# An attention and a feed-forward layer on one core: weight conversion for the first pass moved wholly into the attention stage

## The chip, the cores and the metric

The kernel runs on one core of a Trainium2 chip. The metric is the device time of one execution in microseconds; the time before is the median of three runs. The engines are called as in the profile: PE (TensorE, with PEld for its weight loads), DVE (VectorE), ACT (ScalarE), POOL (GpSimd) and SP (SyncE, which issues all the DMAs here).

## The reference

Random-feature linear attention for 8 batches, 8 heads, 576 tokens and head size 64 is followed by a feed-forward layer over 4608 tokens (model width 512, inner width 2048), all in float32.

```python
def phi(x):
    proj = einsum('bhsd,df->bhsf', x, w_phi)            # 128 features
    proj = proj - max(abs(proj), axis=-1)
    return concatenate([exp(proj), exp(-proj)], axis=-1)
q_p, k_p = phi(q), phi(k)
kv  = einsum('bhsf,bhsd->bhfd', k_p, v);  z = sum(k_p, axis=2)
x   = einsum(q_p, kv) / (einsum(q_p, z) + 1e-6)         # to (4608, 512)
h   = x @ w_in
out = (h * tanh(softplus(h))) @ w_out
```

In the kernel's inputs `w_in` and `w_out` stand as 64-bit words, and the kernel makes float32 pairs (a high and a low part) of them itself: this is the weight conversion.

## The kernel before

**An order written by hand.** Every piece of work is put into a list with a time, `at(time, fn, ...)`, and the list is sorted once. The times set only the order in which each engine, and SP's DMA queue, gets its instructions. What an engine does when is decided on the chip by semaphores.

**Attention.** 36 units of 512 columns each on the key side (`k_*`) and the query side (`q_*`). One step of `STEP` holds key unit u+4 and query unit u. A unit is projected on PE (`k_proj`, `q_proj`, into PSUM tile pp), centred on DVE (`center`: a reduction of the maximum and a subtraction, L204 and L205), and exponentiated on ACT (`k_exp`; for queries after a transpose on PE, `q_turn`, then `q_exp`). `k_sum` adds up kv on PE and `k_store` copies a finished pair out (ACT). `q_num` multiplies by kv on PE; `q_norm` on DVE adds 1e-6 to the denominator (L309), inverts it (L310) and multiplies (L311), each twice a unit; `q_out` transposes on PE, `q_store` copies on ACT and sends x to DRAM (`x_spill`). The last four query units have no key unit beside them; their steps are `TAIL_STEP`.

**Feed-forward.** x is read back in nine chunks of 512 tokens (`x_load`); `x_sum` forms four differences (DVE, L349), and `x_block` makes seven blocks with a high part (ACT, L357) and a low part (DVE, L358). A step (`n`, 72 in all) is one chunk with one of eight pairs of weight blocks (`fp`, numbered 0 to 7): `ff_in` (PE, L374, 42 matmuls), `winograd` (DVE), `mish` and `g_hi` (ACT), `g_lo` (DVE, L415), and `ff_out` (PE, L438, 24 matmuls) for the step before. A segment (`segs`) is a chunk with several pairs in a row; at its end `drain` adds to or starts a partial sum in DRAM. The x blocks are made anew for every segment. `NFIRST` = 4 chunks have their first four pairs in two segments of two steps, the other chunks in one of four.

**Weight conversion.** A piece (`weight_ops`) is a quarter of one pair's `w_in` or `w_out`: five bit operations (absolute, clamp, shift, sign, scale: DVE, the absolute on ACT where not `quiet`), a few POOL operations, one ACT copy (`hi`, L161), and POOL's low part. Eight pieces (pairs 0 and 1) are converted during the attention and stay in SBUF; the eight of pairs 2 and 3 right after it, without pause, into tiles of the pool `late`, whose memory is the attention's until that ends (`close`); the sixteen of pairs 4 to 7 after those, into DRAM (`in_spill`, `out_spill`), from where `again` and `again_out` load them for the second pass. `begin` is the time in the list at which the feed-forward stage proper starts.

Of the kernel before, what the change touches and what calls it, by code (L numbers as in the profile page):

```python
# [16 lines left out]
P = 128  # L17
# [12 lines left out]
SMALL, LARGE = 2.0 ** -15, 1.875 * 2.0 ** 16 - 2.0 ** -7  # L30

LEAD = 4
LEAD_STEP, STEP, TAIL_STEP = 3.0, 7.4, 5.7
FFSTEP = 10.6
HALF = 4
EARLY, SOON, LATER = 22.0, 0.0, 9.0
NFIRST = 4
AHEAD = 2
NXC = 10

# [5 lines left out]
def attention_then_mish(ctx, tc, qT, kT, va, w_phi, w_in, w_out, out):  # L46
# [21 lines left out]
    out_spill = {(fp, k): tc.dram_tile([P, 2, DM], F32, name=f"out_spill_{fp}_{k}")  # L68
                 for fp in range(HALF, NFP) for k in range(2)}

    win, wout, piece = {}, {}, {}

# [26 lines left out]
    def weight_ops(kind, fp, k, quiet):  # L99

        key = (kind, fp, k)
        eng = nc.gpsimd

        def w():
            return piece[key][1][:, 0:4].rearrange("p b m -> p (b m)")

        def absolute():
            words = piece[key][0]
            w8 = ffn.tile([P, 8, P], F32, tag="w8", name=f"w8_{kind}_{fp}_{k}", bufs=2)
            piece[key].append(w8)  # L110
            if quiet:
                nc.vector.tensor_scalar(w().bitcast(U32), words[:, 1], 0x7FFFFFFF, None, op0=ALU.bitwise_and)
            else:
                nc.scalar.activation(w(), words[:, 1].bitcast(F32), AF.Abs)

        def clamp():
            nc.vector.tensor_scalar(w(), w(), LARGE, SMALL, op0=ALU.min, op1=ALU.max)  # L117

        def shift():
            wu = w().bitcast(U32)  # L120
            nc.vector.tensor_scalar(wu, wu, 3, 0x3FFFFFF8, op0=ALU.logical_shift_left, op1=ALU.bitwise_and)

        def sign():
            wu = w().bitcast(U32)
            nc.vector.scalar_tensor_tensor(wu, piece[key][0][:, 1], 0xC0000000, wu, op0=ALU.bitwise_and,  # L125
                                           op1=ALU.bitwise_or)
# [12 lines left out]
        def place():  # L139
            if fp < HALF:  # L140
                resident(fp)
                return win[fp][:, k] if kind == "in" else wout[fp][:, k]
            st = ffn.tile([P, 2, 7 * P], F32R, tag="wst", name=f"wst_{kind}_{fp}_{k}", bufs=1)
            if kind == "in":
                return st.rearrange("p h (b m) -> p h b m", m=P)
            return st[:, :, :DM]

        def total():
            eng.tensor_tensor(w(), w(), piece[key][2], op=ALU.add)  # L149

        def sums(i):
            w8 = piece[key][1]
            a21, a11, a22, a12, s1, s2, s3, s4 = (w8[:, b] for b in range(8))
            o, x, y, op = ((s1, a21, a22, ALU.add), (s2, s1, a11, ALU.subtract), (s3, a11, a21, ALU.subtract),
                           (s4, a12, s2, ALU.subtract))[i]
            eng.tensor_tensor(o, x, y, op=op)  # L156

        def hi():
            dst = place()
            piece[key].append(dst)  # L160
            nc.scalar.copy(dst[:, 0], piece[key][1][:, 1:8] if kind == "in" else w())  # L161

        def lo():
            dst = piece[key][3]
            eng.tensor_sub(dst[:, 1], piece[key][1][:, 1:8], dst[:, 0].bitcast(F32))
            done()

        def rest():
            dst = piece[key][3]
            eng.tensor_sub(w(), w(), dst[:, 0].bitcast(F32))  # L170

        def lo_out():
            dst = piece[key][3]
            eng.tensor_tensor(dst[:, 1], w(), piece[key][2], op=ALU.add)
            done()

        def done():
            dst = piece.pop(key)[3]
            pieces_left.discard(key)
            if fp >= HALF:  # L180
                nc.sync.dma_start(in_spill[fp, k] if kind == "in" else out_spill[fp, k], dst.bitcast(F32))

        ops = [(0.0, absolute), (0.9, clamp), (1.35, shift), (1.8, sign), (2.5, scale)]
        rest_ops = [(2.2, low)]
        if kind == "in":
            rest_ops += [(1.45, total)] + [(0.65, lambda i=i: sums(i)) for i in range(4)] + [(1.6, hi), (2.3, lo)]
        else:
            rest_ops += [(1.3, hi), (1.45, rest), (1.45, lo_out)]
        return ops, rest_ops
# [72 lines left out]
            nc.scalar.copy(kv[p // NHP, p % NHP], kv_ps.pop(p))  # L262


    q_live, x_live, num_live, turned, out_live = {}, {}, {}, {}, {}

    def q_load(n):
        q_live[n] = att.tile([P, 512], F32, tag="qraw", name=f"qraw_{n}", bufs=3)
# [20 lines left out]
    def q_num(n):  # L289
# [3 lines left out]
        for i in range(2):  # L293
# [7 lines left out]
                               start=(t == j == s == 0), stop=(s == 1))  # L301
            num_live[n, i] = ps

    def q_norm(n):
        x = x_live[n]
        for i in range(2):
            ps = num_live.pop((n, i))
            r = att.tile([P, 2, 2], F32, tag="r", name=f"r{i}_{n}", bufs=3)
            nc.vector.tensor_scalar(r, ps[:, :, :, D], 1e-6, None, op0=ALU.add)  # L309
            nc.vector.reciprocal(r, r)  # L310
            nc.vector.tensor_tensor(x[:, i].rearrange("p t (j d) -> p t j d", d=D), ps[:, :, :, :D],  # L311
                                    r.unsqueeze(3).broadcast_to([P, 2, 2, D]), op=ALU.mult)
# [28 lines left out]
    def x_sum(s, i):  # L341
# [130 lines left out]

    for u in range(NU):
        t, after = base(u - LEAD), base(u - LEAD + 1)
        at(t - 1.5 * STEP, k_load, u)
        at(t - 0.8 * STEP, v_load, u)
        at(t, k_proj, u)
        at(t + 0.95, k_center, u)
        at(t + 3.4, k_exp, u)
        at(after + (3.85 if after >= 0 else 0.9), k_sum, u)  # L480
        at(after + (6.3 if after >= 0 else 3.5), k_store, u)
        t, after, end = base(u), base(u + 1), base(u + 2)
        at(t - 1.2 * STEP, q_load, u)
        at(t + 0.95, q_proj, u)
        at(t + 4.9, q_center, u)
        for j in range(2):
            tail = STEP - TAIL_STEP if u + 1 >= NU - LEAD else 0
            at(after + 6.45 + 0.45 * j - tail, q_turn, u, j)
            at(after + 6.9 + 1.2 * j - tail, q_exp, u, j)
        at(end + 1.9, q_num, u)  # L490
        at(end + 3.35, q_norm, u)
        tail = STEP - TAIL_STEP if u + 2 >= NU - LEAD else 0
        at(end + 6.0 - tail, q_out, u)
        at(end + 6.5 - tail, q_store, u)

    begin = base(NU + 2) + 1.0
# [6 lines left out]
    at(begin - 0.5, close)  # L503

    def t_of(n):
        return begin + 5.6 + (n - AHEAD) * FFSTEP if n >= AHEAD else begin - 13.0 + 5.5 * n

    clock = 6.0
    for i, pc in enumerate(pieces):
        quiet = i >= 8  # L510
        if i == 8:
            clock = max(clock, begin + 5.0)
        at(clock - 12.0, weight_load, *pc)
        bits, sums = weight_ops(*pc, quiet)
# [81 lines left out]
```

## Time and profile before

| | us |
|---|---|
| median of three runs | 1110.99 (1110.9 to 1111.02) |
| the profiled execution | 1111.28 |
| its span, first to last instruction | 1109.5 |
| PE busy | 1057.6 |
| DVE busy | 749.3 |
| ACT busy | 489.0 |
| POOL busy | 245.6 |

Busy time is a sum over stages which have different limits. In the 40 slices of the page (27.7 us each) the attention fills about the first eleven; the slices after it up to the 25th hold the conversion beside the feed-forward steps, and from the 26th on POOL does nothing. In a line of a group the last part is the idle time of the engine just before the group, with what ended it. Rows of the timeline have the start, the length, and in brackets the idle time before.

### The profile page before, as it was taken

To read this page: it belongs to the slowest core of one execution; us is meant where nothing else is said; L and a number is where in the kernel's file an instruction comes from. 1 tells how busy PE (TensorE), PEld (TensorE's weight loads), DVE (VectorE), ACT (ScalarE), POOL (GpSimd) and SP (SyncE) were. 2 spreads that over 40 slices of the span, in tenths; PEclk is the share of its full clock that TensorE was granted. 3 is DMA by queue.
4 is the path that set the end of the run, shared out by engine and by line. 5 is a ranking of instruction groups with operands and counts; after the bars stand their busy time and mean duration, and the time that the engine had idled before them with its cause. 6 is when DMAs were issued, how large, how long until landed. Compare 5 with 4: busy or idle time off the path is not lost.

```text
span 1109.5 us, 25630 instructions
## 1 busy us (share of the span) xinstructions
PE 1057.6 (95%) x11200; PEld 958.3 (86%) x11200; DVE 749.3 (68%) x1166; ACT 489.0 (44%) x804; POOL 245.6 (22%) x198
## 2 busy tenths in 40 slices
PE   7899999999888889999999999999999999999998
PEld 6799999999776778879898989999999999999997
DVE  4788878888858987898846757545545545545543
ACT  4666667665544434343435335333323323323331
POOL 0222211111027766543425443000000000000000
PEclk9999999999989989999999999999999999999999
DMA  5535544454223326554341533850230330230221
GB/s 160 170 107 181 162 153 164 151 169 144 87 80 111 131 98 214 214 199 145 121 148 58 175 121 130 338 208 19 95 115 19 96 114 19 96 114 19 96 76 38
DMA packets 62815, 140.29 MB, mean 126 GB/s; under 512 B 4976, under 2 KB 27632, under 8 KB 59376
## 3 DMA queue, kind: packets, MB, share of 16 engines
q1 hardware_dynamic: 62704, 138.66, 36.5%
q8 instruction: 88, 1.44, 0.5%
q14 instruction: 23, 0.19, 0.0%
HBM read 94.60 MB, written 44.04 MB: 125 GB/s over the span
## 4 chain that ended last, share of the span: by engine, by line
PE 52%; DVE 12%; DMA 2%; ACT 2%; POOL 2%; issue 2%; SPq 0%; DVEq 0%; POOLq 0%; ACTq 0%
PE o L438 27%; PE h L374 25%; DVE xc L358 5%; DMA x<-x_spill 2%; DVE xs L349 1%; DVE gl L415 1%; POOL w_in L156 1%; ACT gh L410 1%; DVE u L398 1%; DVE part L446 1%; DVE w_in L125 0%; ACT u L405 0%; POOL t_in L137 0%; DVE w_in L117 0%; POOL w_in L149 0%
## 5 line engine op out<-in xcount | busy, mean ns | idle before, releaser
L374 PEld LDWEIGHTS h<-xc,win 128*128 128x128 f32 x3024 | 383.8, 193 | 37.6 <-issue 15.1
L374 PE MATMUL h<-xc,win 128*128 128x256 f32 x3024 | 392.3, 285 | 20.2 <-DVE u L394 11.9
L438 PE MATMUL o<-wout,gh 128*128 128x512 f32 x1152 | 362.2, 396 | 2.9 <-ACT gh L410 2.9
L438 PEld LDWEIGHTS o<-wout,gh 128*128 128x128 f32 x1152 | 209.9, 191 | 40.0 <-ACT gh L410 3.2
L438 PE MATMUL o<-wout,gl 128*128 128x512 f32 x576 | 226.3, 393 | 4.2 <-DVE gl L415 4.2
L379 ACT COPY p<-h 128x256 f32<-128x256 f32 x72 | 26.8, 372 | 304.1 <-PE h L374 304.1
L386 DVE TENSOR_TENSOR u<-h,p 128x256 f32<-128x256 f32 x72 | 30.4, 422 | 183.8 <-ACT p L379 183.8
L438 PEld LDWEIGHTS o<-wout,gl 128*128 128x128 f32 x576 | 109.6, 190 | 29.1 <-DVE gl L415 5.0
L415 DVE TENSOR_TENSOR gl<-u,gh 128x1024 fp32r<-128x1024 f32 x72 | 93.0, 1292 | 29.1 <-ACT gh L410 29.1
L403 ACT ACTIVATE u<-h 128x256 f32<-128x256 f32 x72 | 27.7, 384 | 149.5 <-PE h L374 144.0
L213 PE MATMUL kvps<-v,e_k 128*64 128x65 f32 x2560 | 83.4, 224 | 4.8 <-ACT e_k L243 4.2
L213 PEld LDWEIGHTS kvps<-v,e_k 128*64 128x64 f32 x2560 | 79.7, 140 | 6.0 <-ACT e_k L243 4.6
L358 DVE TENSOR_TENSOR xc<-x,xc 128x512 fp32r<-128x512 f32 x88 | 75.1, 871 | 11.4 <-ACT xc L357 11.2
L213 PE MATMUL num<-kv,e_q 128*64 128x65 f32 x2304 | 78.4, 223 | 3.4 <-ACT e_q L287 2.7
L213 PEld LDWEIGHTS num<-kv,e_q 128*64 128x64 f32 x2304 | 71.5, 137 | 9.8 <-ACT e_q L287 5.3
L410 ACT CAST gh<-u 128x1024 fp32r<-128x1024 f32 x72 | 75.8, 1052 | 2.2
L287 ACT ACTIVATE e_q<-dt 128x512 f32<-128x512 f32 x144 | 75.5, 613 | 0.1
L398 DVE TENSOR_TENSOR u<-h,u 128x512 f32<-128x512 f32 x72 | 49.3, 685 | 38.5 <-ACT u L403 35.5
L242 ACT ACTIVATE e_k<-e_k 128x1024 f32<-128x1024 f32 x36 | 38.1, 1058 | 76.7 <-DVE e_k L205 76.7
L204 DVE TENSOR_REDUCE m_k<-pp_k 128x8 f32<-128x1024 f32 x36 | 44.0, 1222 | 40.6 <-PE pp_k L198 40.3
L405 ACT ACTIVATE u<-u 128x768 f32<-128x768 f32 x72 | 61.1, 849 | 3.0 <-DVE u L398 3.0
L358 DVE TENSOR_TENSOR xc<-xs,xc 128x512 fp32r<-128x512 f32 x66 | 55.5, 861 | 2.0 <-ACT xc L357 2.0
(62 smaller groups left out, 1166.5 us busy)
## 6 DMA issues: line engine op xcount, KB each, us to landing
x<-x_spill SPq DMA_DIRECT2D x44, 512.0 KB, 5.6
o_part<-part SPq DMA_DIRECT2D x13, 1024.0 KB, 4.8
part<-o_part SPq DMA_DIRECT2D x13, 1024.0 KB, 7.7
v<-va SPq DMA_DIRECT2D x32, 325.0 KB, 3.2
kraw<-kT SPq DMA_DIRECT2D x36, 256.0 KB, 3.9
qraw<-qT SPq DMA_DIRECT2D x36, 256.0 KB, 3.8
x_spill<-xs SPq DMA_DIRECT2D x36, 256.0 KB, 2.7
out<-part SPq DMA_DIRECT2D x36, 256.0 KB, 2.0
```

The costliest lines, as they stand in the source:

```text
L204: nc.vector.tensor_reduce(m, ps, axis=AX.X, op=ALU.max, apply_absolute_value=True)
L213: nc.tensor.matmul(ps[rows], lhsT[:, rows], rhs[h], start=start, stop=stop, skip_group_check=True)
L242: nc.scalar.activation(e[:, :, 1, :], e[:, :, 0, :], AF.Exp)
L287: nc.scalar.activation(e[:, s, :], ps, AF.Exp, scale=2.0 * s - 1.0)
L358: nc.vector.tensor_sub(blk[:, 1], src, blk[:, 0].bitcast(F32))
L374: nc.tensor.matmul(ps, w, x, start=(i in (0, 2) and m == 0), stop=(m == 5), skip_group_check=True)
L386: nc.vector.tensor_tensor(u2, ps[:, 0, 1], u_live[n][0], op=ALU.add)
L398: nc.vector.tensor_tensor(u[:, 1:3], ps[:, 1], u2.unsqueeze(1).broadcast_to([P, 2, CH]), op=ALU.add)
L405: nc.scalar.activation(u[:, 1:4], u[:, 1:4], AF.Mish)
L410: nc.scalar.copy(gh, u_live[n][3])
L415: nc.vector.tensor_tensor(gl, u_live.pop(n)[3], g_live[n][0].bitcast(F32), op=ALU.subtract)
L438: nc.tensor.matmul(ps, g, w, start=(first and f == k == 0), stop=(last and f == 1 and k == 2))
```

## The change

Four things, and new times for the order:

1. All sixteen pieces of pairs 0 to 3 are converted during the attention, one per 14.91 of the list's time. Pairs 2 and 3 go through DRAM and are loaded at `begin` by `again` and `again_out`. The pieces of pairs 4 to 7 start at `begin` + 40.03, with 7.91 between two (before: 9). `NFIRST` is 2, so that there are 20 segments in place of 22.
2. The differences of the first two segments and the low parts of the first segment's blocks are made on POOL.
3. `q_den` on ACT adds 1e-6 (two small instructions a unit); DVE's two reciprocals become one.
4. The last four query units have an order of their own (`T_AT`): a unit's operations follow one another more closely, so that the units overlap differently. In the other steps `k_proj` comes between the two halves of `q_turn`, and `q_den` ahead of `k_exp` on ACT.

```diff
-LEAD_STEP, STEP, TAIL_STEP = 3.0, 7.4, 5.7
+LEAD_STEP = 3.07
+STEP = 7.43
+TAIL_STEP = 5.73
+K_AT = (-0.57, 0.6, 3.04, 3.85, 4.24)
+Q_AT = (0.95, 4.18, 6.45, 6.55, 1.9, 3.04, 5.9, 6.5)
+T_AT = (0.95, 2.0, 4.9, 5.3, 9.0, 10.38, 12.6, 13.1)
+JOIN = 1.0
+PRE = (11.72, 6.53)
+CONV = (12.64, 14.91)
+WORD_AT = 4.77
+X0_AT = (40.59, 30.15)
+RESUME = 40.03
-EARLY, SOON, LATER = 22.0, 0.0, 9.0
-NFIRST = 4
+LATER = 7.91
+NFIRST = 2
...
-                for fp in range(HALF, NFP) for k in range(2)}
+                for fp in range(2, NFP) for k in range(2)}
...
-            if fp < HALF:
+            if fp < 2:
                 resident(fp)
...
-            if fp >= HALF:
+            if fp >= 2:
                 nc.sync.dma_start(in_spill[fp, k] if kind == "in" else out_spill[fp, k], dst.bitcast(F32))
...
+    def q_den(n):
+        r = r_live[n] = att.tile([P, 2, 2, 2], F32, tag="r", name=f"r_{n}", bufs=3)
+        for i in range(2):
+            nc.scalar.activation(r[:, i], num_live[n, i][:, :, :, D], AF.Copy, bias=1e-6)
+
     def q_norm(n):
         x = x_live[n]
+        r = r_live.pop(n)
+        nc.vector.reciprocal(r, r)
         for i in range(2):
             ps = num_live.pop((n, i))
-            r = att.tile([P, 2, 2], F32, tag="r", name=f"r{i}_{n}", bufs=3)
-            nc.vector.tensor_scalar(r, ps[:, :, :, D], 1e-6, None, op0=ALU.add)
-            nc.vector.reciprocal(r, r)
...
-        nc.vector.tensor_tensor(o, a, b, op=ALU.subtract)
+        (nc.gpsimd if s < 2 else nc.vector).tensor_tensor(o, a, b, op=ALU.subtract)
...
-        nc.vector.tensor_sub(blk[:, 1], src, blk[:, 0].bitcast(F32))
+        (nc.vector if s else nc.gpsimd).tensor_tensor(blk[:, 1], src, blk[:, 0].bitcast(F32), op=ALU.subtract)
...
-        at(end + 1.9, q_num, u)
-        at(end + 3.35, q_norm, u)
+        at(end + a[4], q_num, u)
+        at(end + a[5], q_den, u)
+        at(end + a[5] + 0.05, q_norm, u)
...
-        quiet = i >= 8
-        if i == 8:
-            clock = max(clock, begin + 5.0)
+        quiet = i >= 4 * HALF
+        if i == 4 * HALF:
+            clock = max(clock, begin + RESUME)
+        if i < 4 * HALF:
+            clock = CONV[0] + CONV[1] * i
...
+    for fp in (2, 3):
+        at(begin + 0.1 if fp == 2 else begin + 7.6, again, fp)
+        at(begin + 7.4 + 0.1 * fp, again_out, fp)
```

More of the change, by code (lines that the diff above doesn't have):

```diff
@@ L66, in attention_then_mish @@
     in_spill = {(fp, k): tc.dram_tile([P, 2, 7, P], F32, name=f"in_spill_{fp}_{k}")
-                for fp in range(HALF, NFP) for k in range(2)}
+                for fp in range(2, NFP) for k in range(2)}
     out_spill = {(fp, k): tc.dram_tile([P, 2, DM], F32, name=f"out_spill_{fp}_{k}")
-                 for fp in range(HALF, NFP) for k in range(2)}
+                 for fp in range(2, NFP) for k in range(2)}
     win, wout, piece = {}, {}, {}
@@ L262, in k_store @@
             nc.scalar.copy(kv[p // NHP, p % NHP], kv_ps.pop(p))
-    q_live, x_live, num_live, turned, out_live = {}, {}, {}, {}, {}
+    q_live, x_live, num_live, turned, out_live, r_live = {}, {}, {}, {}, {}, {}
     def q_load(n):
@@ L474, in attention_then_mish @@
         t, after = base(u - LEAD), base(u - LEAD + 1)
+        lead = after < 0
         at(t - 1.5 * STEP, k_load, u)
         at(t - 0.8 * STEP, v_load, u)
[L477 to L481, printed above, removed]
-        t, after, end = base(u), base(u + 1), base(u + 2)
+        at(t + K_AT[0], k_proj, u)
+        at(t + K_AT[1], k_center, u)
+        at(t + K_AT[2], k_exp, u)
+        at(after + (0.9 if lead else K_AT[3]), k_sum, u)
+        at(after + (3.5 if lead else K_AT[4]), k_store, u)
+        t, after, end = base(u), base(u + 1), base(u + 2)
+        cut = STEP - TAIL_STEP
+        after -= cut if u == NU - LEAD - 1 else 0.0
+        close_by = end - (cut if u >= NU - LEAD - 2 else 0.0)
+        if u >= NU - LEAD:
+            after = end = close_by = t
+        a = T_AT if u >= NU - LEAD else Q_AT
         at(t - 1.2 * STEP, q_load, u)
-        at(t + 0.95, q_proj, u)
-        at(t + 4.9, q_center, u)
+        at(t + a[0], q_proj, u)
+        at(t + a[1], q_center, u)
         for j in range(2):
-            tail = STEP - TAIL_STEP if u + 1 >= NU - LEAD else 0
-            at(after + 6.45 + 0.45 * j - tail, q_turn, u, j)
-            at(after + 6.9 + 1.2 * j - tail, q_exp, u, j)
-        at(end + 1.9, q_num, u)
-        at(end + 3.35, q_norm, u)
[L492 to L496, printed above, removed]
+            at(after + a[2] + 0.45 * j, q_turn, u, j)
+            at(after + a[3] + 1.2 * j, q_exp, u, j)
+        at(end + a[4], q_num, u)
+        at(end + a[5], q_den, u)
+        at(end + a[5] + 0.05, q_norm, u)
+        at(close_by + a[6], q_out, u)
+        at(close_by + a[7], q_store, u)
+    begin = base(NU + 2) + JOIN
     def close():
@@ L505, in t_of @@
     def t_of(n):
-        return begin + 5.6 + (n - AHEAD) * FFSTEP if n >= AHEAD else begin - 13.0 + 5.5 * n
+        return begin + 5.6 + (n - AHEAD) * FFSTEP if n >= AHEAD else begin - PRE[0] + PRE[1] * n
     clock = 6.0
     for i, pc in enumerate(pieces):
-        quiet = i >= 8
-        if i == 8:
-            clock = max(clock, begin + 5.0)
+        quiet = i >= 4 * HALF
[3 more added lines that the diff above has]
+            clock = CONV[0] + CONV[1] * i
         at(clock - 12.0, weight_load, *pc)
@@ L515, in attention_then_mish @@
         for delay, op in bits:
-            at(clock - 5.0 + delay, op)
+            at(clock - WORD_AT + delay, op)
         for cost, op in sums:
@@ L519, in attention_then_mish @@
             clock += cost
-        clock += EARLY if i < 8 else SOON if i < 16 else LATER
+        clock += LATER
     for s, (sc, fps) in enumerate(segs):
         n = steps.index((s, sc, fps[0], True, fps[0] == fps[-1]))
-        t = t_of(n - 2) if n >= AHEAD + 2 else begin - (45, 20)[s]
+        t = t_of(n - 2) if n >= AHEAD + 2 else begin - (X0_AT[0], 20)[s]
         at(t + 1.0, x_load, s, sc)
@@ L527, in attention_then_mish @@
             at(t + 5.5 + 0.7 * i, x_sum, s, i)
-        t = t_of(n - 1) if n >= AHEAD + 2 else begin - (30, 3.9)[s]
+        t = t_of(n - 1) if n >= AHEAD + 2 else begin - (X0_AT[1], 3.9)[s]
         for b in range(7):
```

2 lines of the change are left out of this document (1 added, 1 removed).

## The prediction

> **What bounds the kernel now.** I read the page first, then the chain of work that ended last, then busy time by stage, and last single stretches in order of time.
>
> ```profile
> span 1109.5 us, 25630 instructions
> PE   7899999999888889999999999999999999999998
> DVE  4788878888858987898846757545545545545543
> PEclk9999999999989989999999999999999999999999
> ```
>
> PE is the bound over most of the span, but it falls to 8 in slices 11 to 15 (27.7 us each), where DVE reaches 9 in slice 14 and the granted clock dips to 8 in slices 12 and 15. What a feed-forward step costs undisturbed is in the end of the chain:
>
> ```profile
> 1082.23 2.15 PE h L374 x18
> 1087.13 2.87 PE h L374 x24
> 1092.75 2.15 PE h L374 x18
> ```
>
> The second halves of two successive steps start at 1082.23 and 1092.75: 10.52 us a step, all of it PE. Step 2, the first after the seam, and the seam's own marks:
>
> ```profile
> 271.88 1.16 PE L198 MATMUL pp_q<-w_phi,qraw 64*128 64x128 f32 x16
> 292.54 1.16 PE L198 MATMUL pp_q<-w_phi,qraw 64*128 64x128 f32 x16
> 319.32 0.73 PE L438 MATMUL o<-wout,gh 128*128 128x512 f32 x2 [2.91 <-ACT gh L410]
> 321.98 0.79 PE L438 MATMUL o<-wout,gl 128*128 128x512 f32 x1 [1.93 <-DVE gl L415]
> 329.57 0.64 PE L374 MATMUL h<-xc,win 128*128 128x256 f32 x4
> ```
>
> Step 2 starts at 329.57 and step 71 at 1087.13: 757.6 us for 69 steps that need 725.9 (69 x 10.52). So the feed-forward stage loses 31.7 us, and this is where:
>
> ```profile
> 329.57:424.25 94.68, 78.64 (x447) 68.42 (x446) 83.39 (x110) 38.96 (x67) 65.49 (x50) 0.93 0.36 126
> 424.25:508.41 84.16, 80.56 (x499) 71.48 (x498) 72.26 (x110) 39.60 (x68) 41.13 (x32) 1.00 0.56 201
> 508.41:676.73 168.32, 165.50 (x1028) 148.41 (x1027) 115.96 (x175) 67.31 (x112) 73.97 (x57) 1.00 0.35 123
> PE h L374 <- DVE u L394: 11.9, 7, 3.8
> ```
>
> A step has 66 matmuls. The first row is nine steps long and holds 447 matmuls, worth 71.3 us: 23.4 lost. There the eight pieces of pairs 2 and 3 are converted without pause beside segments of two steps. DVE is busy 88% of it, the wait under the windows is PE waiting for DVE, and the granted clock is 0.93. The second row (two-step segments, pieces 17.3 apart in the order) loses 4.6 (499 matmuls), the third (mostly four-step segments, same pieces) 4.5 (1028). Their sum, 32.5, agrees with the 31.7.
>
> In the attention the PE is paced by its own work. One unit, without a piece:
>
> ```profile
> 100.30 1.16 PE L198 MATMUL pp_k<-w_phi,kraw 64*128 64x128 f32 x16
> 107.63 1.16 PE L198 MATMUL pp_k<-w_phi,kraw 64*128 64x128 f32 x16
> 108.84 1.23 DVE L204 TENSOR_REDUCE m_k<-pp_k 128x8 f32<-128x1024 f32 x1 [0.91 <-PE pp_k L198]
> 109.61 2.09 PE L213 MATMUL num<-kv,e_q 128*64 128x65 f32 x64
> 111.42 1.06 ACT L242 ACTIVATE e_k<-e_k 128x1024 f32<-128x1024 f32 x1 [2.01 <-DVE e_k L205]
> 112.44 0.42 DVE L311 TENSOR_TENSOR x<-num,r 128x256 f32<-128x256 f32 x1
> 112.51 1.06 ACT L243 ACTIVATE e_k<-e_k 128x1024 f32<-128x1024 f32 x1
> 113.97 0.66 PE L320 MATMUL xt<-ident,x 128*128 128x128 f32 x4
> 114.66 0.59 ACT L327 COPY xs<-xt 128x512 f32<-128x512 f32 x1 [0.83 <-PE xt L320]
> 115.14 2.07 ACT L287 ACTIVATE e_q<-dt 128x512 f32<-128x512 f32 x4
> 115.43 1.16 PE L198 MATMUL pp_k<-w_phi,kraw 64*128 64x128 f32 x16
> ```
>
> A unit takes 7.33 (100.30 to 107.63), or 7.80 with five key tiles in place of four (107.63 to 115.43). DVE has 0.91 idle before the key's reduction (108.84) and ends its normalisation at 112.86, 1.1 us before PE needs it at 113.97; ACT starts the key's exponential at 111.42 after an idle 2.01. Pieces disturb this:
>
> ```profile
> 44.57 1.16 PE L198 MATMUL pp_k<-w_phi,kraw 64*128 64x128 f32 x16
> 264.09 1.16 PE L198 MATMUL pp_k<-w_phi,kraw 64*128 64x128 f32 x16
> L125 DVE SCALAR_TENSOR_TENSOR w_out<-words_out,w_out 128x512 uint32<-128x512 uint32 x3 | 2.1, 694 | 0.1
> L117 DVE TENSOR_SCALAR w_out<-w_out 128x512 f32<-128x512 f32 x3 | 1.3, 421 | 1.4 <-ACT w_out L114 1.4
> L161 ACT CAST win<-w_in 128x896 fp32r<-128x896 f32 x3 | 2.9, 951 | 0.0
> ```
>
> 28 units from 44.57 to 264.09 take 219.5. By the tiles (576 tokens are 4.5 tiles of 128, so 16 of the 36 units have a fifth) 16 are short and 12 long: 16 x 7.33 + 12 x 7.80 = 210.9. The seven pieces in between cost 8.6, or 1.2 each.
>
> **The change part by part.**
>
> *Feed-forward stage.* Pieces of pairs 2 and 3 leave it, the later ones start about three steps after step 2, and only eight steps lie in two-step segments. Two segments fewer also save 14 blocks, 8 differences and 8 drains (DVE), 14 copies (ACT) and eight DMAs. I price what is left by the rates above. From step 2 to the first piece, 34 us, two-step segments without pieces: at most the second row's 4.6 in 84.16, so 1.9. Then 29 us of two-step segments with pieces: 1.6. Then four-step segments: the sixteen pieces take 16 x 16.2 = 259 us in the order, 230 of it here; third row's rate, 4.5 in 168.3, times 17.3/16.2 for the denser pieces: 6.6. Left: 10.1, gain **21.6**. Ends: rates at 0.6 of these, a loss of 6, give a gain of 25.7; twice the rates give 11.6.
>
> *Reload of pairs 2 and 3.* Eight DMAs at the seam (the first row serves the pieces below).
>
> ```profile
> qraw<-qT SPq DMA_DIRECT2D x36, 256.0 KB, 3.8
> win<-in_spill SPq DMA_DIRECT2D x8, 896.0 KB, 6.4
> ```
>
> At 6.4 us each if nothing overlapped, four of them and four smaller ones (512 KB, taken in proportion at 3.7) are 40 us. SP issues pair 2's w_in, then the x load of segment 2, then the rest. Step 4, the first to use pair 2, is two steps and 5.6 us after `begin`, 26.6; two DMAs and an x load are through by then. Pair 3 is due 10.5 later, at 37, and would be up to 8 late if all went one by one. In the second window above the queues moved 201 GB/s; 5.8 MB are 29 us at that. I take 0, with 8 as the upper end. Segment 2's x load queues behind 1.8 MB; DVE's differences wait for it, and PE's output of that step only comes a step later.
>
> *The seam.* From 271.88 (first query unit without a key) to 329.57 are 57.7 us. PE's work in it: 25 of attention (six nums at 1.9, five transposes at 1.0, four projections at 1.0, six of x at 0.5, one key sum at 2.0), two steps' products at 5.02, one step's outputs at 5.5 (the rest of 10.52): 41. So 17 are lost. The waits of 2.91 and 1.93 stay: the order of mish, high and low part is the same. Of the rest, 5.6 lie between the projections at 271.88 and 292.54: three units in 20.7, less the key sum 18.7, for 3 x 4.4 of work. In the new order a unit's centring directly follows its projection, and the first segment's low parts leave DVE for POOL. I take **-6**; ends 0 and -12 (all but the two waits). POOL makes seven low parts and eight differences:
>
> ```profile
> L149 POOL TENSOR_TENSOR w_in<-w_in,t_in 128x512 f32<-128x512 f32 x3 | 3.8, 1275 | 0.2
> ```
>
> At 1.28 the first segment's eleven are 14 us, put 35 to 22 ahead of `begin` and due 11.7 ahead of it; the second's four are 5 us, put 14.5 ahead and due at `begin`. The second segment's x load waits for the first's low parts on SP, with a store of x behind it. Cost 0; if POOL runs late, the first products come up to 5 later.
>
> *Denominator.*
>
> ```profile
> L309 DVE TENSOR_SCALAR r<-num 128x4 f32<-128x4 f32 x72 | 11.1, 154 | 4.4 <-PE num L213 3.4
> L310 DVE RECIPROCAL r<-r 128x4 f32<-128x4 f32 x72 | 12.8, 178 | 2.5
> L262 ACT COPY kv<-kvps 128x260 f32<-128x260 f32 x32 | 11.6, 363 | 1.5 <-PE kvps L213 1.3
> ```
>
> DVE loses two of 154 ns and one of 178: 0.5 us a unit. On ACT, an instruction of four elements lies between the 0.15 of L309 and the 0.36 of a copy of 260; I take 0.2, nearer to the small one, so 0.4 a unit. It stands ahead of the key's exponential and waits for `q_num` (behind it wait the exponential, whose kv sum is a unit later, and the copies): ACT's loop is now num 2.1, den 0.4, two exponentials 2.15, kv copy 0.36, x copy to last query exponential 2.55 (114.66 to 117.21): 7.56. The next num may start 0.35 before its last input is there (three of its sixteen groups), so 7.68 is allowed in a short unit: it fits, by 0.1.
>
> *Pieces in the attention.* Sixteen, one per two units. Three or four bit operations (two at 0.42 taken alike, 0.69, 0.42: 1.55 to 2.0) stand between the key's centring and `q_norm`; the centring starts 0.5 earlier, since `k_proj` has moved ahead of half the transposes, and `q_norm` is 0.5 shorter. This nearly pays for them; the query's centring then ends 0.1 to 0.55 after PE wants its buffer: 0.35 x 16 = 5.6. The ACT copy of an input piece (0.95, L161) stands in the loop that has 0.1 to spare: 0.6 each after the long units' slack, times 8; three of the output pieces 0.4. That is 6.0. Sum 11.6 for 8.6 now: **+3**. Ends: the present 1.2 each, 16 x 1.2 - 8.6 = +10.6; or 0.1 each, -7. SP's spills wait for POOL's low part, with a query load and an x store behind them; query loads go out 1.2 steps or 8.9 ahead in the order and land in 3.8, so 5 of waiting is covered.
>
> *Sum.* 1109.5 - 21.6 - 6 + 3 = 1084.9 of span. The execution profiled was 1111.28, the median 1110.99 is 1.5 above the span: **1086**.
>
> **The rivals.**
>
> *POOL blocks DVE's bit operations.* It happens already:
>
> ```profile
> 373.41 2.33 POOL L165 TENSOR_TENSOR win<-w_in,win 128x896 fp32r<-128x896 f32 x1 [1.79 <-ACT win L161]
> 373.67 2.36 DVE L117 TENSOR_SCALAR w_out<-w_out 128x512 f32<-128x512 f32 x1
> ```
>
> A 0.42 us operation took 2.36 and ended 0.29 after POOL's: 1.94 lost. In the attention POOL's work doubles. If two operations in each of 16 pieces lose 1.94, that is 3.9, of which DVE's idle 0.9 in each of two units absorbs 1.8: 2.1 more than the 0.7 a piece of my sum, 2.8 x 16 - 8.6 = +36 in place of +3, and the time is 1120: slower. It decides at 2.4 a piece all told (16 of them 38 us, 30 more than the 8.6 paid now). Against it: L117 kept 421 ns in the attention, and a piece's POOL work ends in the order before the next piece's bits begin. 0.05. The Trainium skill, "SBUF — State Buffer", section "SBUF: two separate sides", says that DVE and GpSimd hold one port pair as an exclusive lock for a whole instruction; the two rows agree; whether the new pieces meet POOL's at all no run here shows.
>
> *ACT paces the attention.* At 0.36 for each den the loop is 7.88, 0.2 over, 6.4 in 32 units, and pieces at 1.2: +17 in place of +3, 1100. The 2.01 idle of ACT speaks against, its new place behind num for. 0.12.
>
> *The stage keeps its losses*, through late reloads or drains and x loads of short segments: half the gain, 1097. 0.10.
>
> *Better*: pieces at 0.5, seam -10, 6 lost after it: 1109.5 - 25.7 - 10 - 0.6 + 1.5 = 1075. 0.13.
>
> *No change* (within 0.2%, which a measurement of this kernel can just tell): the gains only move into the attention. 0.02.
>
> **How the numbers follow.** My forecast (1080 to 1093) has 0.58. From the better case to the ACT case, 1073 to 1101, leaves out little but the blocked DVE. Faster 0.93, same 0.02, slower 0.05.
>
> **What would show it.** In the changed profile: units still 7.33 or 7.80 without a piece, and about 0.7 more where one falls; ACT's first exponential right behind the den; DVE well under 9 in slices 12 to 17 and a clock of 1.0 there; step 71 less step 2 about 736; no PE wait for a reload at step 4 or 5. Wrong is the forecast if bit operations of the attention take 1 us or more, if units sit at 7.9 without pieces, or if the nine steps after the seam still lose over 15.

## The result and the profile after

| | before | after |
|---|---|---|
| median, four runs each | 1110.95 us | 1077.21 us (1076.65 to 1079.47) |
| ratio of the times, 95% interval | | 0.9706 (0.9686 to 0.9726) |
| profiled execution, and its span | 1111.28, 1109.5 | 1079.47, 1077.7 |
| first query unit without a key, start | 271.88 | 272.79 (+0.9) |
| from there to step 2 (the seam) | 57.69 | 51.19 (-6.5) |
| step 2 to step 71 | 757.56 | 731.35 (-26.2) |
| step 71 to the end | 22.4 | 22.4 |

The three differences add up to the 31.8 us by which the spans differ. The page after, in its rows of slices (26.9 us each):

```profile
PE   6999999999989989999999999999999999999998
...
DVE  4878888888645786585684653544545545555543
...
PEclk9999999999989999999999999999999999999999
```

PE is at 9 from the second slice on, but for the 8 of slices 12 and 15 and of the last. Slices 12 to 17 of DVE read 4 5 7 8 6 5 where before they read 5 8 9 8 7 8. The granted clock still reads 8 in slice 12, the seam, where the prediction had 1.0. Busy time by stage, in stretches of the lengths used before (busy time and count of each engine, granted clock, DMA share, GB/s):

```profile
323.98:418.66 94.68, 91.50 (x574) 83.14 (x573) 66.42 (x104) 38.94 (x66) 34.07 (x28) 0.98 0.56 204
418.66:502.82 84.16, 84.16 (x529) 76.16 (x528) 56.06 (x90) 36.16 (x61) 39.80 (x30) 1.00 0.39 135
502.82:671.14 168.32, 166.14 (x1036) 149.44 (x1035) 98.12 (x156) 68.56 (x115) 51.04 (x39) 1.00 0.32 114
```

Counted as in the prediction, 574 matmuls at 10.52 us for 66 are 91.5: the first stretch loses 3.2 us, where it lost 23.4 (by the starts of the steps, 4.9 and 24.8). The second stretch loses nothing. Two rows are all that the lists of PE's waits hold, in the first and in the third stretch:

```profile
PE h L389 <- ACT xc L372: 3.2, 1, 3.2
...
PE h L389 <- DVE u L409: 2.2, 2, 1.5
```

The 3.2 goes back to one late x load, in order of time:

```profile
375.26 0.69 DVE L364 TENSOR_TENSOR xs<-x 128x512 f32<-128x512 f32 x1 [5.07 <-DMA x<-x_spill]
```

DVE idles 5.07 us for it; the differences (this row), the conversion's operations between them and then ACT's copies come late, and PE waits. The load's first half had gone out at 366.31. On SP's queue a piece's spill stands ahead of it, and that waits for POOL's low part, which ends at 365.74; beside this same POOL operation two low parts of DVE took 3.21 us, where one alone takes 0.68. Which of the two made the load late, no run isolates.

In the attention, a unit of after (PE, and the small new ACT work) and then of before (PE; its `pp_k` at 100.30 and 107.63 stand in the prediction):

```profile
198.14 0.17 ACT L318 ACTIVATE r<-num 128x4 f32<-128x4 f32 x1 [0.76 <-PE num L224]
198.21 1.05 ACT L253 ACTIVATE e_k<-e_k 128x1024 f32<-128x1024 f32 x1
...
200.85 0.60 PE L292 MATMUL dt<-ident,e_q 128*128 128x128 f32 x4
...
201.38 1.16 PE L209 MATMUL pp_k<-w_phi,kraw 64*128 64x128 f32 x16
...
202.47 0.66 PE L292 MATMUL dt<-ident,e_q 128*128 128x128 f32 x4
...
203.06 1.16 PE L209 MATMUL pp_q<-w_phi,qraw 64*128 64x128 f32 x16
...
204.15 2.09 PE L224 MATMUL num<-kv,e_q 128*64 128x65 f32 x64
...
209.06 1.16 PE L209 MATMUL pp_k<-w_phi,kraw 64*128 64x128 f32 x16
```

```profile
99.33 1.04 PE L281 MATMUL dt<-ident,e_q 128*128 128x128 f32 x8
...
102.28 2.09 PE L213 MATMUL num<-kv,e_q 128*64 128x65 f32 x64
```

Before, eight transposes, both projections and then num: 99.33 to 102.28, 2.95 us. After, four transposes, `k_proj`, four transposes, `q_proj`, num: 200.85 to 204.15, 3.30 us for the same instructions. A short unit now takes 7.68 (201.38 to 209.06) and not 7.33, with a piece beside it or not. PE's waits between 50 and 250 us are one row:

```profile
PE kvps L224 <- issue: 0.7, 1, 0.7
```

So PE waits for no engine there. The 28 units, in order of time:

```profile
42.42 1.16 PE L209 MATMUL pp_k<-w_phi,kraw 64*128 64x128 f32 x16
...
264.21 1.16 PE L209 MATMUL pp_k<-w_phi,kraw 64*128 64x128 f32 x16
```

They take 221.8, and 16 x 7.68 + 12 x 8.15 = 220.7: the longer units cost 9.8 (28 x 0.35), and 1.1 is left for all pieces together. That 1.1 lies in the third and fourth unit alone; every other one takes 7.68 or 8.15 within 0.01, with a piece or without.

The seam's two waits:

```profile
310.86 3.45 PE L389 MATMUL h<-xc,win 128*128 128x256 f32 x18 [1.93 <-DVE u L409]
...
317.24 0.50 PE L453 MATMUL o<-wout,gl 128*128 128x512 f32 x1 [2.08 <-DVE gl L430]
```

These are not the two that the prediction had. Its 2.91 for ACT's high part is gone, its 1.93 for DVE's low part is the 2.08 here, and the 1.93 here is new: it stands ahead of the second half of step 1's products and is for DVE's sums `u`.

### The profile page after: what moved, and what is told of

Same layout as the page of the kernel before. It is cut to its first block, busy times and chain, and to the rows that moved or that the text cites. A ratio compares the mean times of both kernels' runs of the same rounds, so it can differ in the third digit from the quotient of the medians.

```text
span 1077.7 us, 25575 instructions
## 1 busy us (share of the span) xinstructions
PE 1052.4 (98%) x11200; PEld 954.6 (89%) x11200; DVE 671.0 (62%) x1005; ACT 497.8 (46%) x870; POOL 250.7 (23%) x213
## 4 chain that ended last, share of the span: by engine, by line
PE 91%; DVE 4%; ACT 2%; DMA 1%; issue 1%; POOL 0%; SPq 0%; DVEq 0%; ACTq 0%
PE o L453 34%; PE h L389 32%; PE kvps L224 7%; PE num L224 6%; PE pp_k L209 3%; PE pp_q L209 3%; PE dt L292 3%; PE xt L335 2%; DVE xc L373 2%; DMA x<-x_spill 1%; ACT e_q L298 1%; DVE gl L430 0%; DMA kraw<-kT 0%; DVE u L413 0%; ACT e_k L253 0%
## 5 line engine op out<-in xcount | busy, mean ns | idle before, releaser
L389 PE MATMUL h<-xc,win 128*128 128x256 f32 x3024 | 388.1, 284 | 7.3 <-DVE u L409 4.1
L394 ACT COPY p<-h 128x256 f32<-128x256 f32 x72 | 26.8, 373 | 298.2 <-PE h L389 298.2
L453 PEld LDWEIGHTS o<-wout,gl 128*128 128x128 f32 x576 | 108.6, 189 | 26.9 <-DVE gl L430 3.2
L413 DVE TENSOR_TENSOR u<-h,u 128x512 f32<-128x512 f32 x72 | 49.4, 686 | 49.7 <-ACT u L418 48.6
L224 PE MATMUL num<-kv,e_q 128*64 128x65 f32 x2304 | 75.9, 223 | 0.5 <-ACT e_q L298 0.5
L373 DVE TENSOR_TENSOR xc<-x,xc 128x512 fp32r<-128x512 f32 x76 | 57.3, 771 | 8.4 <-ACT xc L372 8.3
L215 DVE TENSOR_REDUCE m_q<-pp_q 128x8 f32<-128x1024 f32 x36 | 43.8, 1216 | 7.3 <-PE pp_q L209 7.3
L209 PE MATMUL pp_k<-w_phi,kraw 64*128 64x128 f32 x576 | 43.2, 292 | 4.5 <-DMA kraw<-kT 4.5
```

Source lines behind the costliest of these rows:

```text
L209: nc.tensor.matmul(ps[:, j, n], raw[rows, n * P:(n + 1) * P], w_phi2[rows], start=True, stop=True)
L215: nc.vector.tensor_reduce(m, ps, axis=AX.X, op=ALU.max, apply_absolute_value=True)
L224: nc.tensor.matmul(ps[rows], lhsT[:, rows], rhs[h], start=start, stop=stop, skip_group_check=True)
L373: (nc.vector if s else nc.gpsimd).tensor_tensor(blk[:, 1], src, blk[:, 0].bitcast(F32), op=ALU.subtract)
L389: nc.tensor.matmul(ps, w, x, start=(i in (0, 2) and m == 0), stop=(m == 5), skip_group_check=True)
L413: nc.vector.tensor_tensor(u[:, 1:3], ps[:, 1], u2.unsqueeze(1).broadcast_to([P, 2, CH]), op=ALU.add)
```

## The experiments

The two theories after this reading. *Switch and cover*: going between 64-row projections and 128-row transposes twice more a unit costs PE 0.35, and the longer unit hides the pieces. *Ordinary pieces* (the prediction's): the pieces cost by themselves, and `k_proj`'s new place is free. The other experiments take the parts one by one. All times are medians of four or five executions (nine for e2), in five rounds; the kernel before ran at 1109.46 beside e1, e2, e5 and e6, at 1111.36 beside e3, e4, e8 and e10, and at 1109.66 beside e7, e9 and e11.

| kernel | us | ratio to before, 95% |
|---|---|---|
| e1, after, `k_proj` back behind the transposes | 1078.23 | 0.971 (0.9692 to 0.9727) |
| e2, before, `k_proj` between the transposes | 1115.94 | 1.0046 (1.0031 to 1.0062) |
| e10, e1 and bit operations behind the centring | 1068.56 | 0.9623 (0.9602 to 0.9644) |
| e6, before, first part of the change alone | 1093.91 | 0.9849 (0.9832 to 0.9865) |
| e5, after, old order of the last units | 1084.84 | 0.977 (0.9754 to 0.9786) |
| e4, after, first x work on DVE | 1083.14 | 0.9746 (0.9728 to 0.9763) |
| e3, after, den on DVE | 1077.48 | 0.9695 (0.9676 to 0.9714) |
| e7, after, `NFIRST` 4 | 1087.15 | 0.9793 (0.9771 to 0.9815) |
| e9, after, no pause before the late pieces | 1090.61 | 0.9828 (0.9811 to 0.9846) |
| e8, after, bit operations where POOL works | 1086.62 | 0.9778 (0.9758 to 0.9797) |
| e11, e10 and an earlier step 0 | 1065.50 | 0.96 (0.9586 to 0.9614) |

**e1: the switch taken out of the changed kernel.**

```diff
-K_AT = (-0.57, 0.6, 3.04, 3.85, 4.24)
+K_AT = (-0.5, 0.6, 3.04, 3.85, 4.24)
```

> The changed kernel (1077.2) with the key projection put back behind both halves of the query transpose. Theory 'switch': the units of 7.67 and 8.15 are PE's own work, because going from the transposes (128 rows) to a projection (64 rows) and back twice a unit costs 0.35 more than once. Then units without a piece return to 7.33 and 7.80, the 32 units give back 11 us, and what the pieces and the den then cost comes out of that: 1066 if they cost nothing, 1071 to 1074 if they cost the 11.6 us of the prediction. Theory 'latency': the units are paced by the loop over num, den, exponential and query exponential, which the early key projection shortens; then PE waits in place of switching and the time is 1077 or more. Theory 'cover': the 0.35 is what hides the pieces, so all of it comes back as waits: 1076 to 1078.

The time is that of after. The list of e1's PE waits, 50 to 250 us, is led by a row that after's had not; below it, two of its units in order of time:

```profile
PE pp_q L209 <- DVE e_q L216: 1.6, 5, 0.3
```

```profile
193.60 1.16 PE L209 MATMUL pp_k<-w_phi,kraw 64*128 64x128 f32 x16
...
195.09 1.16 PE L209 MATMUL pp_q<-w_phi,qraw 64*128 64x128 f32 x16 [0.32 <-DVE e_q L216]
...
202.00 1.16 PE L209 MATMUL pp_k<-w_phi,kraw 64*128 64x128 f32 x16
...
208.10 0.42 DVE L142 TENSOR_SCALAR t_in<-w_in 128x512 uint32<-128x512 uint32 x1
...
208.43 1.22 DVE L215 TENSOR_REDUCE m_q<-pp_q 128x8 f32<-128x1024 f32 x1
...
209.48 1.16 PE L209 MATMUL pp_k<-w_phi,kraw 64*128 64x128 f32 x16
```

The unit from 202.00 to 209.48 takes 7.48, so the switch is gone, but the one ahead of it takes 8.40, 0.60 more than a long unit's 7.80. A piece's last bit operation (L142, 208.10) stands ahead of the query's maximum (208.43); the centring ends late, and the next `q_proj` waits for its buffer (again 0.32, at 210.96). The 28 units take 221.0, 0.8 less than in after: what the switch gave back is lost again, which is *cover*. The listed waits are far less than these 10.1 over 210.9. A unit with a wait of 0.32 is 0.60 longer, and some 4.7 of the 10.1 fall into the first six units, for which the list has single waits of other kinds; e10 tests what the pieces cost.

**e2: the switch alone, in the kernel before.**

```diff
-        at(t, k_proj, u)
+        at(t - 0.7, k_proj, u)
```

> The kernel before (1111.0) with one edit: the key projection is put between the two halves of the query transpose. 'Switch': units of 7.68 and 8.15 in this kernel too, 28 of them 9.8 us longer, less whatever the longer unit hides of the seven pieces' 8.6: 1113 to 1122. 'Latency': the earlier centring helps the pieces and nothing gets longer: 1103 to 1111.

Three starts of `k_proj` in order of time:

```profile
100.48 1.16 PE L198 MATMUL pp_k<-w_phi,kraw 64*128 64x128 f32 x16
...
108.16 1.16 PE L198 MATMUL pp_k<-w_phi,kraw 64*128 64x128 f32 x16
...
116.31 1.16 PE L198 MATMUL pp_k<-w_phi,kraw 64*128 64x128 f32 x16
```

Units of 7.68 and 8.15, as in after, and a slower kernel. All 28 take 223.1 (43.69 to 266.79), 3.6 more than before's 219.5: of the 9.8 for the longer units, 6.2 are made up by pieces that cost less beside them, so the cover shows here too. The Trainium skill, "TensorEngine Tiling (Array Packing)", section "Key Properties", says that a change of tiling mode drains TensorE; the 0.35 agrees with that, but no run here changed the shapes themselves.

**e10: neither cost.** On top of e1, a piece's last two bit operations go behind the query's centring.

```diff
-K_AT = (-0.57, 0.6, 3.04, 3.85, 4.24)
+K_AT = (-0.5, 0.6, 3.04, 3.85, 4.24)
-        ops = [(0.0, absolute), (0.9, clamp), (1.35, shift), (1.8, sign), (2.5, scale)]
-        rest_ops = [(2.2, low)]
+        late_bits = (1.8, 2.5) if quiet else (3.8, 3.9)
+        ops = [(0.0, absolute), (0.9, clamp), (1.35, shift), (late_bits[0], sign), (late_bits[1], scale)]
+        rest_ops = [(2.2 if quiet or kind == "in" else 2.5, low)]
```

> The kernel with the key projection behind both transposes (1078.2), and with the last two bit operations of a piece put behind the query's centring in place of ahead of it (the output pieces' copy one place later on ACT). In that kernel a pair of units with a piece took 7.48 + 8.39 = 15.87, or 7.61 + 7.80, against 7.33 + 7.80 = 15.13, and PE waited for the query's centring (0.32). If that wait is what the pieces cost, 0.6 to 0.74 of a pair come back, 14 pairs: 1068 to 1071. If the cost is ACT's (copies of the pieces, den): 1076 to 1079.

Two units of e10 in order of time:

```profile
193.96 1.16 PE L210 MATMUL pp_k<-w_phi,kraw 64*128 64x128 f32 x16
...
200.59 1.22 DVE L217 TENSOR_TENSOR e_q<-pp_q,m_q 128x1024 f32<-128x1024 f32 x1
...
201.29 1.16 PE L210 MATMUL pp_k<-w_phi,kraw 64*128 64x128 f32 x16
...
201.73 0.68 DVE L136 SCALAR_TENSOR_TENSOR w_in<-words_in,w_in 128x512 uint32<-128x512 uint32 x1
...
208.62 1.16 PE L210 MATMUL pp_k<-w_phi,kraw 64*128 64x128 f32 x16
```

The piece's fourth operation (201.73) follows the centring (200.59), and both units take 7.33, as a unit of before does without a piece. The 28 units take 213.25, where e1's take 221.0 and after's 221.8, and the median falls by 8.6 against after. The pieces' price was in the main the late centring, as the prediction said; the switch hid it at a price as high.

**e6: the first part of the change alone.** In the kernel before: `NFIRST` 2, `LATER` 7.91, pairs 2 and 3 through DRAM with their reload, and

```diff
+        if i == 16:
+            clock = max(clock, begin + 40.03)
+        if i < 16:
+            clock = 12.6 + 14.85 * i
...
-        clock += EARLY if i < 8 else SOON if i < 16 else LATER
+        clock += LATER
```

> The kernel before with only the move of the pieces (sixteen in the attention, pairs 2 and 3 through DRAM, two chunks in two segments, later start and spacing of the rest); den, x sums, the order of a unit and of the last query units as before. If the feed-forward stage's gain of 26 us is that move's, step 2 to step 71 takes 731 to 736 here as in the changed kernel. For the attention: the present 1.2 us a piece gives 16 x 1.2 = 19, 10.6 more than before, and the time 1111 - 26 + 11 = 1096; if the pieces cost nothing, 1078 to 1085; if POOL's doubled work blocks DVE's bit operations, over 1100.

Step 2 to step 71 takes 730.7: the whole gain of the feed-forward stage, 26.8, is this part's. But the 28 units take 229.8, 10.3 more than before. The largest row of PE's waits, 50 to 250 us, and the end of a piece's bit operations in order of time:

```profile
PE xt L320 <- DVE r L309: 5.9, 12, 0.8
```

```profile
162.95 0.43 DVE L131 TENSOR_SCALAR t_in<-w_in 128x512 uint32<-128x512 uint32 x1
163.29 0.15 DVE L309 TENSOR_SCALAR r<-num 128x4 f32<-128x4 f32 x1
...
164.27 0.41 PE L320 MATMUL xt<-ident,x 128*128 128x128 f32 x2 [0.72 <-DVE r L309]
```

The fourth bit operation starts at 162.95, the first denominator stands behind it on DVE, and PE's transposes wait 0.72 for `q_norm`. So the other parts of the change gave 8.0 us of attention and 5.9 of seam (57.05 here). Taking back den's engine alone (e3) or `k_proj`'s place alone (e1) loses none of the 8.0; which of the new times earn it was not separated.

**e5 and e4: the seam.** After with the old order for the last four units and the old times of the first two feed-forward steps (`PRE`); and the order of after with the x work of the first segments on DVE.

```diff
-T_AT = (0.95, 2.0, 4.9, 5.3, 9.0, 10.38, 12.6, 13.1)
+T_AT = (0.95, 4.18, 10.48, 10.58, 13.36, 14.5, 15.66, 16.26)
-PRE = (11.72, 6.53)
+PRE = (13.0, 5.5)
```

> The changed kernel with the times of the last four query units, and of the first two feed-forward steps, as before. If the seam's gain of 6.5 us (57.7 to 51.2 from the first query unit without a key to step 2) comes from the new order of these units: 1083 to 1085. If it comes from the low parts and the conversion having left DVE there: 1077 to 1079.

```diff
-        (nc.gpsimd if s < 2 else nc.vector).tensor_tensor(o, a, b, op=ALU.subtract)
+        nc.vector.tensor_tensor(o, a, b, op=ALU.subtract)
...
-        (nc.vector if s else nc.gpsimd).tensor_tensor(blk[:, 1], src, blk[:, 0].bitcast(F32), op=ALU.subtract)
+        nc.vector.tensor_tensor(blk[:, 1], src, blk[:, 0].bitcast(F32), op=ALU.subtract)
```

> The changed kernel with the first eight differences and the first segment's seven low parts back on DVE. They are about 8 x 0.7 + 7 x 0.7 = 10.5 us of DVE in the last units. If DVE has room there: 1076.5 to 1078.5. If the seam's gain rests on POOL doing them: up to the 6.5 us of the seam, 1080 to 1084.

First the marks and one wait of e5, then those of e4:

```profile
274.46 1.16 PE L209 MATMUL pp_q<-w_phi,qraw 64*128 64x128 f32 x16
...
298.91 0.77 PE L335 MATMUL xt<-ident,x 128*128 128x128 f32 x4 [1.04 <-DVE x L326]
...
330.61 3.04 PE L389 MATMUL h<-xc,win 128*128 128x256 f32 x24
```

```profile
273.16 1.16 PE L209 MATMUL pp_q<-w_phi,qraw 64*128 64x128 f32 x16
...
295.42 1.06 PE L292 MATMUL dt<-ident,e_q 128*128 128x128 f32 x8 [1.98 <-DVE e_q L216]
...
327.75 2.44 PE L389 MATMUL h<-xc,win 128*128 128x256 f32 x19
```

The seam takes 56.15 with the old order and 54.59 with DVE's x work, against 51.19 with both parts and 57.05 with neither (e6). Alone, POOL's help gives 0.9 and the order 2.5; together 5.9. Each is one profiled execution, and kernels with after's seam (after, e1, e3, e7, e8, e10) have 49.4 to 51.6 there, so the 0.9 may be nothing. That the two need each other shows better in the medians: taking one back alone costs 7.6 us in e5 and 5.9 in e4, each about what the whole seam gained. In e5 three transposes wait 1.04 each for a normalisation, where a unit's steps stand farther apart in the list; in e4 the closer order is held up by DVE (1.98 for the centring).

**e3: the denominator on DVE again, in its new place.**

```diff
-            nc.scalar.activation(r[:, i], num_live[n, i][:, :, :, D], AF.Copy, bias=1e-6)
+            nc.vector.tensor_scalar(r[:, i], num_live[n, i][:, :, :, D], 1e-6, None, op0=ALU.add)
```

> The changed kernel (1077.2) with the addition of 1e-6 back on DVE (two small instructions, one merged reciprocal as in the change). If the den on ACT is needed to keep DVE in time: units with a piece get up to 0.3 longer, 16 x 0.3 = 5, 1080 to 1083. If a unit's PE work (7.67 and 8.15 with the key projection between the transposes) covers either place: 1076.5 to 1078. If the den on ACT costs, because ACT's exponential waits for num behind it: 1073 to 1076.

The same time as after, with units of 7.68 and 8.15. With PE's unit that long, the engine of the denominator doesn't matter. Whether it would in e10, where the units are short, was not tried.

**e7: short segments again.** `NFIRST` is 4, all else as in after.

> The changed kernel (1077.2) with four chunks in two segments of two steps, as before, so 22 segments in place of 20. The prediction's rates (two-step segments with pieces lose 4.6 in 84 us, four-step ones 4.5 in 168) give 8 steps at 2.3 us more: 1079 to 1081. If DVE's load in those steps is not what PE waited for before, but the dense pieces: 1076.5 to 1078. The last steps also run four chunks later with pairs 2 and 3, so their reload has more time.

Step 2 to step 71 takes 737.9, a loss of 12.0 in place of 5.5, and the median is 10 higher: two more two-step chunks beside pieces cost 6.5 in the profiled execution, the fastest of four (1083.67 to 1090.26). Both expected ranges were too low.

**e9: the late pieces without their pause.**

```diff
-RESUME = 40.03
+RESUME = 5.0
```

> The changed kernel with the pieces of pairs 4 to 7 starting 5 after the stage begins in place of 40, at the same spacing. If the pause keeps DVE free where the two-step segments need it: 35 us more of them with pieces, at the rate of 4.6 in 84, 2 us, and POOL's work beside the seam's blocks 1 to 3: 1079 to 1082. If the pause is worth nothing: 1076.5 to 1078. If the reload DMAs and the words' loads collide on the queue, step 4 or 5 waits: over 1082.

SP's queue, DVE and PE in order of time:

```profile
329.00 1.36 SPq L103 DMA_DIRECT2D wout<-out_spill  x2
...
330.40 0.69 SPq L107 DMA_DIRECT2D words_in<-w_in  x1
...
342.99 0.43 DVE L123 TENSOR_SCALAR w_in<-words_in 128x512 uint32<-128x512 uint32 x1 [6.54 <-DMA words_in<-w_in]
...
344.36 2.04 PE L389 MATMUL h<-xc,win 128*128 128x256 f32 x8 [6.02 <-DVE u L409]
```

The words of the next piece are issued at 330.40, behind an x load and the last six of the reload's eight DMAs (325.56 to 330.36; the row at 329.00 is the last pair), and DVE can use them at 342.99, 12.6 later. DVE waits 6.54, with the steps' own work behind that operation, and PE waits 6.02. The stage loses 14.6, 9.1 more than in after, and 8.2 of that before step 4, so the third expectation is the one that came. What the prediction took as a free reload is free because no piece's words are queued behind it: that is the pause's doing.

**e8: the rival of POOL's block, made to happen.** The piece's bit operations are put where POOL still works on another piece.

```diff
-        ops = [(0.0, absolute), (0.9, clamp), (1.35, shift), (1.8, sign), (2.5, scale)]
+        ab, dv = (0.0, 0.0) if quiet else (-7.43, -3.23)
+        ops = [(ab, absolute), (0.9 + dv, clamp), (1.35 + dv, shift), (1.8 + dv, sign), (2.5 + dv, scale)]
...
-        at(clock - 12.0, weight_load, *pc)
+        at(clock - (20.0 if i < 16 else 12.0), weight_load, *pc)
```

> The changed kernel with the four bit operations of the attention's pieces put behind the query's centring of the unit before (the absolute a unit earlier still), where for the eight input pieces POOL is at work on the 2.08 us low part of the piece before, while for the eight output pieces it is not. If POOL's work holds DVE's operation up until it ends: one operation of nearly every input piece takes 1.5 to 2.2 us in place of 0.42, the output pieces' stay at 0.42 to 0.5; the key's centring behind it is then late by up to 1.7 us, and the time 1080 to 1092. If both engines share without waiting: all operations at 0.42, and 1077 to 1080.

The clamp in the groups by line, 50 to 250 us, first in after, then in e8:

```profile
L128 DVE TENSOR_SCALAR w_in<-w_in 128x512 f32<-128x512 f32 x6 | 2.8, 472 | 0.0
```

```profile
L128 DVE TENSOR_SCALAR w_in<-w_in 128x512 f32<-128x512 f32 x6 | 10.8, 1799 | 0.0
```

1799 ns in place of 472, and the 28 units take 231.0, 9.2 more. One of these clamps and POOL's low part of the piece before, in order of time:

```profile
192.43 2.09 POOL L176 TENSOR_TENSOR wst_in<-w_in,wst_in 128x896 fp32r<-128x896 f32 x1 [7.84 <-ACT wst_in L172]
192.62 2.19 DVE L128 TENSOR_SCALAR w_in<-w_in 128x512 f32<-128x512 f32 x1
```

The clamp ends 0.29 after POOL. Eight clamps of the attention meet POOL so, two of them of output pieces that follow an input piece, which the expectation had not counted; each takes 1.91 to 2.19. The units around 192 and 210 us with such a meeting take 8.80 in place of 7.68, and two short units with a piece that doesn't meet POOL keep 7.68. So the rival was real, and the change's order keeps out of its way: no bit operation of after's attention takes over 0.8.

**e11: the better version, with one of the seam's waits attacked.** On top of e10, `mish`, high and low part of step 0 come earlier in the list:

```diff
-        at(second + 0.8 if n >= AHEAD else begin - 2.0 + 2 * n, mish, n, 0)
-        at(after + 0.9, mish, n, 1)
-        at(after + 1.8, g_hi, n)
-        at(after + (3.7 if n >= AHEAD else 2.8), g_lo, n)
+        at(second + 0.8 if n >= AHEAD else begin if n else begin - 4.6, mish, n, 0)
+        at(after + 0.9 if n else begin - 4.3, mish, n, 1)
+        at(after + 1.8 if n else begin - 4.2, g_hi, n)
+        at(after + (3.7 if n >= AHEAD else 2.8) if n else begin - 2.2, g_lo, n)
```

> The kernel with the bits behind the query's centring (1068.6), and at the seam the first step's mish ahead of the second step's first copy on ACT, its high part right after, and its low part on DVE ahead of the second segment's blocks. In the changed kernel PE waited 2.08 for that low part and worked at a clock of 0.86 around it. If that order is what delays the low part: the wait goes, step 2 starts 3 to 5 us earlier, 1064 to 1066. If the second segment's blocks then are what PE waits for (they are made later): 1067 to 1069.

PE in order of time:

```profile
263.76 1.16 PE L210 MATMUL pp_q<-w_phi,qraw 64*128 64x128 f32 x16
...
301.83 3.67 PE L390 MATMUL h<-xc,win 128*128 128x256 f32 x18 [1.93 <-DVE u L410]
...
305.30 0.89 PE L454 MATMUL o<-wout,gh 128*128 128x512 f32 x2
```

The outputs at 305.30 follow the products without a wait, since their high and low parts are now made during those. The wait of 1.93, which the edit leaves alone, stays. The seam takes 47.3 (step 2 starts at 311.03), where e10's takes 50.1; at 1065.50 this is the fastest kernel, 4.0% under before.

## Why the prediction was right, and where it was not

The sign held, and the size nearly: 1086 forecast, 1077.2 measured. That lies below the 1080 to 1093 to which the prediction gave 0.58, and inside its wider 1073 to 1101, nearest to the better case of 1075 (0.13). Of that case the stage's gain came (25.7 there), and its seam of -10 did not. The 9 us between are four pieces: 4.6 of the stage, 2.1 of the attention, 0.5 of the seam and 2.0 of the step from span to median.

*Feed-forward stage*, 21.6 forecast and 26.2 measured. The cause was named rightly (e6 alone gives 26.8), but three terms of the sum were off. The first is the need, "69 x 10.52". Step 2 takes only 7.8 in both kernels (329.6 to 337.3, 324.0 to 331.8), since one half of a step's outputs is missing in it. So the stage lost about 34 before and loses 8 now, where 31.7 and 10.1 stand in the sum; this alone is some 2.6 of the 4.6.

The second is "third row's rate, 4.5 in 168.3, times 17.3/16.2", 6.6 for 230 us of four-step segments: by the starts of the steps they lose 3.1 now, from step 8 to step 32. The row was no mixture, though the prediction calls it "mostly" four-step: it holds steps 16 to 32, all of them in four-step segments. It was a few lumps read as a rate. Before, 1.8, 1.2 and 1.0 were lost in steps 20, 24 and 28, the first steps of segments; now nothing is lost in steps 12, 16 and 20, and 0.9 and 1.7 in steps 24 and 28. Nor does DVE's busy share tell where: it was 0.69 in the row of before (116.0 of 168.3), and is 0.67 in the stretch of now that loses nothing. Why one such step is free beside pieces and another is not, no run isolates.

The third term, 3.5 for the 63 us of two-step segments, is near by luck. They lose 4.9, all at one late x load (a wait of 3.2 and slower products behind it) and none at the rate that was priced. Counting matmuls shows 3.2 there, since it takes a step's 42 of the products and 24 of the outputs as equally long. The three together, 2.6 and 3.5 less 1.4, are the 4.6 but for rounding. In e7, where two more chunks are in two-step segments beside pieces, 84 us of them cost 6.5, where the two rates differ by 2.3 (4.6 less half of 4.5).

*Attention*, +3 forecast and +0.9 measured, with the wrong working. The 28 units take 2.3 more, and the way from the last of them to the first query unit without a key 0.8 more; the 42 us ahead of them, which the sum does not have, take 2.1 less, and no run isolates why. "The centring starts 0.5 earlier, since `k_proj` has moved ahead of half the transposes" counted the move's benefit and not its price: 0.35 in each of 28 units, 9.8 (e2). And the pieces, 0.7 each in the sum, cost almost nothing, since those longer units cover them (e1, e2). So the sum came near because two errors cancel. The mechanism for the pieces was right where they aren't covered: the centring ends late for PE's buffer (e1), and what is put behind it is free (e10). The mark that was named, units of 7.33 and about 0.7 more with a piece, is wrong for after, where units take 7.68 with a piece or without. The upper end, the old price for every piece, +10.6, is what the moved pieces give without the other parts: +10.3 (e6). That old price, 1.2 each, is itself too high: the second of before's 28 units (51.90 to 61.72) is 2.0 over its 7.80, and PE waits in it 0.8 and 0.6 for nothing that the profile shows, ahead of a piece's first operation on DVE (59.62).

*Denominator*: it takes 0.17 (198.14) where the sum had 0.2, and the key's first exponential is right behind it (198.21), as said; in the time its engine has no weight (e3). ACT as the pace, 0.12, did not come.

*Seam*, -6 and -6.5: right, with both reasons given there, and e4 and e5 show that each needs the other. "The waits of 2.91 and 1.93 stay" did not hold, though 1.93 and 2.08 are left: the first of these is for other work than either wait of before, and that it has the size of one is chance.

*Reload*, 0 taken, 0 found: no wait for a pair's weights is in the first stretch's list. The reason given was the queue's capacity; e9 shows that the pause counts as well, since what is queued behind the reload comes late. The x load that the prediction let queue there was in time; a later one was not, and cost the wait of 3.2.

*POOL's block*, 0.05: it did not happen in the attention, and e8 shows that it could have. The price for it was 36 us, with two operations in each of sixteen pieces; e8, where one operation in eight pieces meets POOL, paid 9.2.

*Median against span*: 1.5 above was carried over from before; of after, the slowest of four executions was profiled, and the median is 0.5 below its span. That is 2.0 of the 9.

## What to carry to other kernels

When an instruction is moved on the engine that is the bound, count the changes of shape on that engine as well as the waits: the same matmuls in another order took 0.35 us a unit more. Side work on an engine that feeds the bound belongs behind the operation that the bound waits for (e10), and its price can be hidden by a cost elsewhere, so taking back one part alone may show nothing (e1). A loss that comes in a few lumps is no rate: look at which steps lose before carrying it to another stretch.

## What the runs showed of the hardware

Two more changes a unit between 64-row projections and 128-row transposes cost PE 0.35 us, with no wait for any engine in its list. In after the eight transposes take 1.12 in two halves (200.85 to 201.38, 202.47 to 203.06) and the two groups of sixteen projections 1.09 each (201.38 to 202.47, 203.06 to 204.15); in before the transposes take 0.97 in a row (99.33 to 100.30) and both groups 1.98 (100.30 to 102.28). That this price and the pieces' hide each other so fully (after and e1 are 1 us apart) was not in the prediction's sum.

A DVE bit operation of 0.42 that meets POOL's low part ends 0.29 after it: 2.36 long in before (373.67) and 2.19 in e8 (192.62).
